# Two experts' gathered rows and a doubled identity moved into buffers that outlive the first stage

## The chip, the cores and the metric

The kernel runs on one core of one Trainium2 chip. A time is device microseconds of one execution. The time before is the median of three timed executions; one more execution was recorded by the hardware profiler, and all rows shown here come from that one.

## The reference

Two blocks follow one another. The first is a recurrent attention (RWKV-7) over 768 steps for 4 batches and 8 heads of width 40; its output is seen as 3072 rows of 320 numbers. The second sends each row to the best of 8 experts, keeps at most 80 rows for an expert (those with the largest gate) and writes the result to the rows' own places.

```python
for t in range(S):
    y[:, :, t] = einsum('bhd,bhde->bhe', rt, state)
    Sa = einsum('bhde,bhe->bhd', state, at)
    state = state * wt - einsum('bhd,bhe->bhde', Sa, bt) + einsum('bhd,bhe->bhde', vt, kt)
...
logits = x @ w_gate
expert_idx = argmax(logits, axis=1)      # gate_w: the softmax value of that expert
for e in range(E):                       # E = 8, capacity = 80
    tok_idx = where(expert_idx == e)[0]  # cut to the 80 largest gate_w
    h = maximum(x[tok_idx] @ w1[e], 0.0)     # 320 -> 1024
    out[tok_idx] = gate_w[tok_idx, None] * (h @ w2[e])   # 1024 -> 320
```

## The kernel before

**First stage.** The recurrence is cut into 24 units (12 blocks of 64 steps, two pairs of batches). For each group of four units a small triangular matrix is inverted in 30 steps; the first group's inversion is done by VectorE, the other five by GpSimd (POOL). The order of all instructions in this stage is written by a planner (`Plan`): each step is given with its engine, a duration, the keys that it reads and writes, and the planner lists the steps greedily by the time at which they could start. Keys such as `("kb", 16)` or `("lt", 5)` name a buffer and the unit or group that uses it. Buffers are rings: `kb` has ten of 1024 columns, so unit 16's is `kb_6`, unit 18's `kb_8`, unit 23's `kb_3`. These ten buffers and a few more belong to the pool `keep`, which lasts until the end. When their units are done, the weights of experts 0 and 1 are loaded into them (`early_weights`, L966 to L982, issued by SyncE, SP): expert 0 uses `kb_4` to `kb_8`, expert 1 `kb_9` and `kb_0` to `kb_3`. Their second layers fill 960 columns of `kb_6`, 640 of `kb_8`, and 640 of `kb_3`. Finished rows of x go to the DRAM tensor `x_rows`.

**Second stage** (L1014 to L1084). The 80 places of each expert are found: `idx_g` (L1077) holds the row numbers for fetching, `idx_s` (L1082) those for writing back. TensorE runs matmuls of no use for the result among this, 22 (`WARM`, L1074) and, behind the last useful one, 16 (`AFTER`, L1084); they read tiles of the pool `sl`.

**Third stage** (L1087 on). The pool `fs` is opened, in memory that the earlier pools gave back. The order in this stage isn't written by hand: each engine's queue is ordered by a list scheduler, which takes an instruction when its operands and its buffer are there by its own estimate, the earlier in the program first. POOL copies the identity twice into `pair` (L1094, L1095), used at L1154. `gather(e)` (L1097) is an indirect DMA issued by POOL that fetches an expert's rows. `turn_x` turns them (two copies `twice` on ScalarE, three transposes on TensorE, the copy `xe` on VectorE), `first_layer` (L1125, L1131) and `second_layer` (L1144) are the matmuls, `turn_y` turns back, scales by the gate that lies in the fetched row's last column (L1156) and scatters by an indirect DMA of POOL (L1157). For each e the program has: `first_layer(e)`, `turn_x(e+1)`, `turn_y(e-2)`, `gather(e+2)`, `second_layer(e-1)`; `gather(0)` to `gather(3)` stand ahead of the loop. The tag `rows` has four buffers, so that `gather(4)` takes that of expert 0.

The weights of experts 2 and 3 are loaded whole by SP (L1004 to L1007) when the first stage ends. Those of experts 4 to 7 follow in ten pieces each (L1177). A piece waits until the piece three before it has landed: SP stores one word of it (`behind`, L1167), and so waits. The fourth piece and all later ones also come after a word of expert 0's fetched rows.

Of the kernel before, what the change touches and what calls it, by code (L numbers as in the profile page):

```python
# [8 lines left out]
F32 = mybir.dt.float32  # L9
# [8 lines left out]
class Plan:  # L18
# [6 lines left out]
    def add(self, eng, us, lag, when, fn, reads=(), writes=(), psum=None, to=(), dma=0.0, sooner=0.0):  # L25
        o = dict(eng=eng, us=us, lag=lag, when=when, fn=fn, i=len(self.ops), deps=set(), psum=None,
                 reads=list(reads), writes=list(writes), to=list(to), dma=dma, sooner=sooner)
        if psum:
            key, n = psum
            if key not in self.width:  # L30
                self.width[key] = n
                o["psum"] = key
            o["writes"].append(key)
        for key in o["reads"]:
            for p, wrote in self.touch.get(key, ()):
                if wrote:
                    o["deps"].add(p)
        for key in o["writes"]:
            for p, _ in self.touch.get(key, ()):
                o["deps"].add(p)  # L40
        for key in o["reads"]:
            self.touch.setdefault(key, []).append((o["i"], False))
        for key in o["writes"]:
            self.touch.setdefault(key, []).append((o["i"], True))
        self.ops.append(o)
# [101 lines left out]
def kernel(  # L147
# [19 lines left out]
    nc = tc.nc  # L167
    B, H, S, D = r.shape
    N, DM = out.shape
    E = moe_w_gate.shape[1]  # L170
    F = moe_w1.shape[2]
    cap = min(int(moe_capacity), N)
    T, C, HB = 64, 32, 64
    NCI = S // T
    NP = B // 2
    NM = NCI * NP
    GU = 4
# [4 lines left out]
    XW = DM + 1  # L182
# [12 lines left out]
    ident = const.tile([128, 128], F32, name="ident")  # L195
# [13 lines left out]
    def view(t, offset, *dims):  # L209
        return bass.AP(t.tensor, t.offset + offset, [list(t.ap[0])] + [list(d) for d in dims])  # L210

    LOOK = 10
# [7 lines left out]
                kb=1024, psi=512, VL=4 * BV, UL=H * X, iv=H * SEG + 1, ivc=512, ends=H * SEG + 1, bT=512, kT=512, rv=1024,  # L220
                lt=C * C, ltT=C * C, gt=512, W=H * X, sT=DM + HB - D, st0=4 * BS, st1=4 * BS, xT=512, xg=GU * XW,
# [4 lines left out]
    keep_ = ctx.enter_context(tc.tile_pool(name="keep", bufs=1))  # L226
    KEPT = [("ah", NM - 10), ("ah", NM - 5), ("ah", NM - 8)] + [("kb", n) for n in range(LOOK)]
    kept = {(n, i % LOOK): keep_.tile([128, COLS[n]], F32, name=f"{n}_{i % LOOK}") for n, i in KEPT}
    weights = {}
    with ExitStack() as p1:  # L230
        hold = p1.enter_context(tc.tile_pool(name="hold", bufs=1))
# [20 lines left out]
        add = plan.add  # L252
# [713 lines left out]
        def early_weights(e):  # L966
            ks = range(NM - 10 + 5 * e, NM - 5 + 5 * e)
            kbs = [at("kb", n) for n in ks]
            rest = at("ah", ks[0])
            w2s = [kbs[2 + i][:, 0 : DM * c].rearrange("p (c d) -> p c d", d=DM) for i, c in enumerate((3, 3, 2))]  # L970
            weights[e] = kbs[0:2], rest, [w2s[f // 3][:, f % 3, :] for f in range(FK)]

            def go():
                for i in range(2):
                    nc.sync.dma_start(kbs[i], moe_w1[e, 128 * i : 128 * i + 128, :])
                for j in range(2):
                    nc.sync.dma_start(rest[64 * j : 64 * j + 64], moe_w1[e, KW:, FH * j : FH * j + FH])
                for i, o in enumerate(w2s):
                    c = o.shape[1]
                    nc.sync.dma_start(o, moe_w2[e, 384 * i : 384 * i + 128 * c, :].rearrange("(c p) d -> p c d", p=128))  # L980
            add("SP", 4.5, 2.0, 0.0, go, [("tops", 0)],
                [("kb", n) for n in ks] + [("ah", ks[0])], dma=7.5)  # L982

        for e in range(2):
            early_weights(e)
        rank_late()
# [100 lines left out]
    fs = ctx.enter_context(tc.tile_pool(name="fs", bufs=2))  # L1087
# [2 lines left out]
    ps_t = ctx.enter_context(tc.tile_pool(name="ps_t", bufs=1, space=PSUM))  # L1090
    ps_y = ctx.enter_context(tc.tile_pool(name="ps_y", bufs=1, space=PSUM))
    rows, xes, hts, yts = {}, {}, {}, {}
    pair = fs.tile([128, HB], F32, name="pair", tag="pair", bufs=1)
    nc.gpsimd.tensor_copy(pair[0:HB], ident[0:HB, 0:HB])  # L1094
    nc.gpsimd.tensor_copy(pair[HB:], ident[HB:, HB:])  # L1095

    def gather(e):  # L1097
        rows[e] = fs.tile([cap, XW], F32, name="rows", tag="rows", bufs=4)
        nc.gpsimd.indirect_dma_start(
            out=rows[e][:, 0:XW], out_offset=None, in_=x_dram[:, :],  # L1100
            in_offset=bass.IndirectOffsetOnAxis(ap=idx_g[:, e : e + 1], axis=0))
# [47 lines left out]
    def turn_y(e):  # L1149
        yT = yts.pop(e)  # L1150
        yq = ps_t.tile([cap, DM], F32, name="yq", tag="yq")
        for i in range(2):
# [6 lines left out]
            in_=y[:, :], element_offset=0, bounds_check=N - 1, oob_is_err=False, in_offset=None)  # L1159

    gather(0)
    words = []

# [6 lines left out]
    for e in range(1, 4):  # L1170
        gather(e)
# [24 lines left out]
    for e in range(E + 1):  # L1196
        if e < E:
            first_layer(e)
        if e + 1 < E:
            turn_x(e + 1)  # L1200
        if e > 1:
            turn_y(e - 2)
            if e + 2 < E:
                gather(e + 2)
        if e > 0:
            second_layer(e - 1)
# [27 lines left out]
```

## Time and profile before

| | us |
|---|---|
| timed executions | 541.29, 542.07, 542.22 (median 542.07) |
| profiled execution, whole | 537.84 |
| its span, first to last instruction | 536.1 |
| TensorE busy, of the span | 406.9 (76%) |
| VectorE busy | 312.1 (58%) |
| GpSimd busy | 225.8 (42%) |
| ScalarE busy | 181.1 (34%) |
| mean granted TensorE clock | 0.902 of full |

The clock has two levels here, 1.0 (2.4 GHz) and 0.5 (1.2 GHz); a value between is a mean over a stretch that has both. Busy shares are means over three stages with different limits. The page's chain of work that ended last reaches back only to the last scatter, so the stages have to be read from the timeline.

### The profile page before, as it was taken

How to read it: one execution, taken by the hardware profiler on the slowest of the kernel's cores; microseconds unless marked ns; L12 is line 12 of the kernel's file. 1: busy time of each engine (PE TensorE's matmuls, PEld its weight loads, DVE VectorE, ACT ScalarE, POOL GpSimd, SP SyncE). 2: the span in 40 equal slices, each digit the busy share in tenths (PEclk: the TensorE clock that was granted, in tenths of full speed). 3: DMA queues.
4: the chain of work that ended last, by engine and by line, in shares of the span. 5: the costliest groups of instructions: out<-in, count | busy, mean ns of one | idle time of the engine just before them, and what ended most of it. 6: DMA issues, size and time to landing. Idle time of an engine off the chain costs nothing. (4 is left out here: it accounts for less than half of the span.)

```text
span 536.1 us, 24562 instructions
## 1 busy us (share of the span) xinstructions
PE 406.9 (76%) x10807; PEld 348.9 (65%) x10807; DVE 312.1 (58%) x706; ACT 181.1 (34%) x353; POOL 225.8 (42%) x395
## 2 busy tenths in 40 slices
PE   2746069987946999898799998989889601699895
PEld 1535058866735877787677877878678501398885
DVE  5867976725720855694575843668567898312212
ACT  2333045453431454346255454343523100010100
POOL 8010011489878701398889930897000000202122
PEclk9988559998975999899999999999979955789999
DMA  9776457667686278567766666333720498676660
GB/s 132 114 112 123 80 132 115 119 101 148 101 237 125 41 175 155 130 129 146 141 153 118 149 152 121 70 75 51 162 73 17 119 321 279 195 220 189 208 199 27
DMA packets 243035, 73.08 MB, mean 136 GB/s; under 512 B 218464, under 2 KB 236272, under 8 KB 242928
## 3 DMA queue, kind: packets, MB, share of 16 engines
q1 hardware_dynamic: 213008, 65.50, 54.2%
q10 hardware_dynamic: 29152, 4.36, 5.3%
q8 instruction: 85, 1.39, 1.1%
q0 software_dynamic: 768, 1.64, 1.1%
q14 instruction: 22, 0.18, 0.1%
HBM read 53.26 MB, written 18.13 MB: 133 GB/s over the span
## 5 line engine op out<-in xcount | busy, mean ns | idle before, releaser
L505 POOL TENSOR_TENSOR tmp<-lt 128x30 f32<-128x30 f32 (+9 forms) x150 | 84.9, 566 | 59.1 <-DMA lt<-blocks 48.4
L507 POOL TENSOR_TENSOR lt<-lt,tmp 128x30 f32<-128x30 f32 (+9 forms) x150 | 90.1, 600 | 11.8
L714 DVE TENSOR_TENSOR UL<-ps,mask 128x832 f32<-128x832 f32 x24 | 24.5, 1021 | 51.9 <-PE ps L709 51.9
L765 PE MATMUL ps<-wsel,xT 128*128 128x192 f32 x192 | 39.1, 349 | 2.3 <-DVE xT L755 1.4
L376 DVE TENSOR_TENSOR_SCAN P<-dec,begins 128x520 f32<-128x520 f32 x24 | 31.5, 1321 | 9.7 <-ACT dec L372 9.6
L351 PE MATMUL ps<-ident,raww 128*128 128x128 f32 x88 | 16.7, 321 | 26.0 <-DMA raww<-in_w_dram 24.8
L765 PEld LDWEIGHTS ps<-wsel,xT 128*128 128x128 f32 x192 | 32.6, 200 | 4.4 <-DVE xT L755 1.7
L351 PE MATMUL ps<-ident,kb 128*128 128x128 f32 x192 | 31.7, 290 | 4.5 <-DVE kb L414 2.6
L742 DVE TENSOR_TENSOR st<-ps,st 128x832 f32<-128x832 f32 (+1 forms) x24 | 23.8, 992 | 18.8 <-PE ps L731 18.7
L492 POOL MEMSET nt<- 32x1024 f32 x12 | 11.3, 945 | 54.6 <-ACT nt L424 54.1
L384 DVE TENSOR_TENSOR_SCAN iv<-dec,ends 128x520 f32<-128x520 f32 x24 | 30.4, 1267 | 4.1 <-ACT ivc L403 3.5
L351 PEld LDWEIGHTS ps<-ident,raww 128*128 128x128 f32 x88 | 11.3, 162 | 28.1 <-DMA raww<-in_w_dram 15.9
L459 DVE TENSOR_TENSOR psi<-ps,mask 128x512 f32<-128x512 f32 x24 | 16.4, 686 | 21.8 <-PE ps L444 20.7
L1157 POOL DMA_INDIRECT out_dram<-y,idx_s x8 | 7.5, 932 | 50.9 <-DVE y L1156 34.9
L618 ACT COPY rv<-ps 128x1024 f32<-128x1024 f32 x24 | 24.4, 1015 | 11.7 <-PE ps L351 11.0
L414 DVE TENSOR_TENSOR kb<-rawkb,ps 128x640 f32<-128x640 f32 x22 | 17.9, 813 | 17.2 <-PE ps L351 11.1
L351 PEld LDWEIGHTS ps<-ident,kb 128*128 128x128 f32 x192 | 22.0, 146 | 8.2 <-issue 3.5
L696 ACT COPY W<-ps 128x832 f32<-128x832 f32 x24 | 20.5, 854 | 14.3 <-PE ps L691 7.4
L731 PE MATMUL ps<-UL,kb 64*64 64x104 f32 (+1 forms) x768 | 23.2, 261 | 2.7 <-DVE UL L714 2.7
L662 PE MATMUL ps<-VL,psi 64*64 64x104 f32 x768 | 24.6, 268 | 0.4 <-DVE VL L635 0.3
L709 PE MATMUL ps<-W,nt 64*64 64x104 f32 x768 | 23.3, 258 | 2.1 <-DVE lb L874 1.9
L351 PE MATMUL ps<-ident,rawr 128*128 128x128 f32 x96 | 16.1, 292 | 10.8 <-DVE ah L394 10.3
(186 smaller groups left out, 951.3 us busy)
## 6 DMA issues: line engine op xcount, KB each, us to landing
w<-in_moe_w_dram SPq DMA_DIRECT2D x16, 320.0 KB
w<-in_moe_w_dram SPq DMA_DIRECT2D x16, 256.0 KB
VL<-in_v_dram SPq DMA_DIRECT2D x96, 40.0 KB
out_dram<-zero SPq DMA_DIRECT2D x8, 480.0 KB
raww<-in_w_dram SPq DMA_DIRECT2D x44, 80.0 KB
rawkb<-in_k_dram SPq DMA_DIRECT2D x44, 80.0 KB
rawkb<-in_b_dram SPq DMA_DIRECT2D x44, 80.0 KB
rawr<-in_r_dram ACTq DMA_DIRECT2D x84, 40.0 KB
```

The costliest lines, as they stand in the source:

```text
L351: nc.tensor.matmul(o, lhsT=i, rhs=ident, start=True, stop=True, is_transpose=True, skip_group_check=True)
L376: nc.vector.tensor_tensor_scan(at("P", n), at("dec", n)[:, 0 : H * SEG], begins, 0.0, op0=Alu.mult, op1=Alu.add)
L384: nc.vector.tensor_tensor_scan(at("iv", n)[:, H * SEG : 0 : -1], at("dec", n)[:, H * SEG : 0 : -1], at("ends", n)[:, H * SEG : 0 : -1], 0. ...
L505: e.tensor_tensor(out=tv, in0=t3[:, 0:s, s : s + 1].to_broadcast([128, s, n]), in1=t3[:, s : s + 1, s + 1 :].to_broadcast([128, s, n]), op ...
L507: e.tensor_tensor(out=t3[:, 0:s, s + 1 :], in0=t3[:, 0:s, s + 1 :], in1=tv, op=Alu.add)
L618: nc.scalar.copy(at("rv", n).rearrange("p (k c) -> p k c", k=2), ps[:, bank(kr) : bank(kr) + 2, :])
L662: nc.tensor.matmul(ps[T * x : T * x + T, b0 + q, X * i : X * i + X], lhsT=psi[rows, q, i, :], rhs=at("VL", n)[rows, vo : vo + X], start=i ...
L709: nc.tensor.matmul(ps[T * bb : T * bb + T, b0 + q, X * i : X * i + X], lhsT=tm[rows, q, i, :], rhs=at("W", n)[rows, wo : wo + X], start=Tr ...
L714: nc.vector.tensor_tensor(out=view(at("UL", n), 0, (M4 * X, 2), (1, M4 * X)), in0=view(ps[:, bank(ku), :], 0, (512, 2), (1, M4 * X)), in1= ...
L731: nc.tensor.matmul(ps[HB * q : HB * q + HB, b0 + bb, yo + lo : yo + hi], lhsT=at("kb", n)[rows, o : o + HB], rhs=at(name, n)[rows, vo + lo ...
L742: nc.vector.tensor_tensor(out=view(st, o, (BS, M4), (step, 2), (1, n_)), in0=view(flat, 512 * bank(ky) + o, (4 * T, M4), (step, 2), (1, n_ ...
L765: nc.tensor.matmul(ps[:, b0, WS * m : WS * m + WX], lhsT=at("xT", n)[:, 2 * T * cof(m, 0) : 2 * T * cof(m, 0) + 2 * T], rhs=wsel_[:, WS * ...
```

## The change

`pair` becomes 64 columns (960 to 1023) of `kb_6`, and the two copies into it become a step of the first stage's plan, on POOL, that reads `("lt", 5)`, the matrix of the last inversion, and writes `("kb", 16)`. It is given to the planner ahead of `early_weights`. The rows of expert 0 are fetched into columns 640 to 960 of `kb_8`, those of expert 1 into the same columns of `kb_3`. Experts 2 to 7 keep the tag `rows` with its four buffers.

```diff
@@ -226,6 +226,7 @@
     kept = {(n, i % LOOK): keep_.tile([128, COLS[n]], F32, name=f"{n}_{i % LOOK}") for n, i in KEPT}
+    pair = kept["kb", (NM - 8) % LOOK][:, 3 * DM : 3 * DM + HB]
     weights = {}
@@ -981,6 +982,12 @@
+        def doubled():
+            for q in range(2):
+                rows_ = slice(HB * q, HB * q + HB)
+                nc.gpsimd.tensor_copy(pair[rows_], ident[rows_, rows_])
+
+        add("POOL", 0.5, 0.1, 0.0, doubled, [("lt", NM // GU - 1)], [("kb", NM - 8)])
         for e in range(2):
             early_weights(e)
@@ -1090,12 +1097,12 @@
     rows, xes, hts, yts = {}, {}, {}, {}
-    pair = fs.tile([128, HB], F32, name="pair", tag="pair", bufs=1)
-    nc.gpsimd.tensor_copy(pair[0:HB], ident[0:HB, 0:HB])
-    nc.gpsimd.tensor_copy(pair[HB:], ident[HB:, HB:])
 
     def gather(e):
-        rows[e] = fs.tile([cap, XW], F32, name="rows", tag="rows", bufs=4)
+        if e < 2:
+            rows[e] = kept["kb", (NM - 6 + 5 * e) % LOOK][0:cap, 2 * DM : 2 * DM + XW]
+        else:
+            rows[e] = fs.tile([cap, XW], F32, name="rows", tag="rows", bufs=4)
```

## Rows read from the trace of the kernel before

**Rows 1.** Busy time in two stretches; then granted clock, DMA share, GB/s.

```profile
460.00:480.00 20.00, 15.23 (x292) 12.74 (x292) 2.64 (x10) 2.34 (x10) 4.32 (x6) 0.83 0.60 188
480.00:500.00 20.00, 18.52 (x492) 17.10 (x487) 3.90 (x10) 1.73 (x7) 3.71 (x4) 1.00 0.62 191
```

**Rows 2.** Timeline from 460 us: start, duration, engine, line; idle before in brackets.

```profile
460.74 0.17 DVE L1077 TENSOR_SCALAR idx_g<-row 80x8 int32<-80x8 f32 x1
460.84 2.76 PE L1084 MATMUL ids_p<-sel,ones_b 128*128 128x384 bf16 x16
463.83 0.23 POOL L1094 COPY pair<-ident 64x64 f32<-64x64 f32 x1 [18.98 <-PE ids_p L1084]
...
464.69 1.13 POOL L1099 DMA_INDIRECT rows<-x_rows,idx_g  x1 [0.36 <-POOL pair L1095]
```

**Rows 3.** Waits of 440 to 537 us: total, times, longest.

```profile
POOL pair L1094 <- PE ids_p L1084: 19.0, 1, 19.0
```

**Rows 4.** Timeline: first transposes, first layer of expert 0, that of expert 3.

```profile
467.69 0.50 PE L1110 MATMUL xp<-ident,rows 80*128 80x80 f32 x2 [4.09 <-DMA rows<-x_rows,idx_g]
...
469.00 4.11 PE L1125 MATMUL hp<-xe,kb 128*64 128x80 f32 x64 [0.50 <-DVE xe L1113]
...
488.58 2.39 PE L1125 MATMUL hp<-xe,w 128*64 128x80 f32 x63
```

**Rows 5.** Timeline: VectorE's result and the indirect DMA that waits for it.

```profile
492.60 0.55 DVE L1156 TENSOR_SCALAR y<-yq,rows 80x320 f32<-80x320 f32 x1
...
493.42 0.94 POOL L1157 DMA_INDIRECT out_dram<-y,idx_s  x1 [5.73 <-DVE y L1156]
```

**Rows 6.** Short stretches, as Rows 1: the last three columns are clock, DMA share, GB/s.

```profile
462.50:463.00 0.50, 0.50 (x5) 0.31 (x4) 0.00 (x0) 0.00 (x0) 0.00 (x0) 1.00 0.46 164
...
465.00:466.00 1.00, 0.00 (x0) 0.00 (x0) 0.00 (x0) 0.00 (x0) 0.82 (x1) 0.84 0.00 0
466.00:467.00 1.00, 0.00 (x0) 0.00 (x0) 0.00 (x0) 0.00 (x0) 0.87 (x1) 0.50 0.33 96
...
472.00:473.00 1.00, 1.00 (x24) 0.94 (x20) 0.00 (x0) 0.00 (x0) 0.00 (x0) 0.74 0.53 125
```

**Rows 7.** The tile `rows`: the eight gathers' time from issue to landing.

```profile
DMA to landing us min/median/max: 2.9/4.1/4.7
```

**Rows 8.** Timeline: last use of unit 16's keys; POOL around the last inversion's end.

```profile
341.45 0.89 PE L731 MATMUL ps<-UL,kb 64*64 64x104 f32 x32
...
373.03 0.16 POOL L519 MEMSET lt<- 128x32 f32 x1
384.66 0.21 POOL L816 COPY xg<-gsm 128x4 f32<-128x4 f32 x1 [11.47 <-DVE gsm L813]
```

**Rows 9.** Timeline: early weights' issue; last expert's weights and the matmuls that use them.

```profile
424.96 2.31 SPq L980 DMA_DIRECT2D kb<-in_moe_w_dram  x3
...
516.79 0.22 SPq L1167 DMA_DIRECT2D word<-w1r  x1
...
521.82 1.12 PE L1131 MATMUL hp<-xe,w1r 64*64 64x80 f32 x32
```

**Rows 10.** Stretches near the end of the first stage, columns as Rows 6.

```profile
388.00:390.00 2.00, 0.43 (x15) 0.46 (x19) 1.10 (x6) 0.19 (x1) 0.00 (x0) 1.00 0.34 54
390.00:392.00 2.00, 2.00 (x73) 1.80 (x66) 1.90 (x9) 0.28 (x1) 0.00 (x0) 0.65 0.97 329
```

**Rows 11.** Timeline: matmuls of L1074, behind L1070 in the program, ahead of it here.

```profile
453.89 4.36 PE L1074 MATMUL warm<-sel,ones_b 128*128 128x384 bf16 x13
```

**Rows 12.** Timeline: ScalarE's queue, and the second layer that needs its result.

```profile
491.48 0.39 ACT L1107 COPY twice<-rows 80x64 f32<-80x64 f32 x2 [7.11 <-DMA rows<-x_rows,idx_g]
...
491.78 0.44 ACT L1134 ACTIVATE hT<-hp 128x320 f32<-128x320 f32 x1
...
500.38 2.77 PE L1144 MATMUL yp<-hT,w 128*64 128x80 f32 x71
...
507.80 0.39 ACT L1107 COPY twice<-rows 80x64 f32<-80x64 f32 x2 [7.52 <-DMA rows<-x_rows,idx_g]
```

## Prediction, made before the changed kernel was run

> **What bounds the kernel now.** The page comes first, but its chain of work that ended last stops at the last scatter, and its busy shares are means over three stages. So I cut the span into stretches and looked for the ones that the change touches. In the expert stage TensorE is the limit once it runs: it is busy 18.52 of 20 us from 480 on, and only 15.23 of 20 between 460 and 480, at a mean clock of 0.83 [rows 1]. Time lost at that stage's start is lost at the end too, since everything behind it is TensorE's own work. The timeline of the start shows the loss. The row numbers `idx_g` are ready at 460.74 + 0.17 = 460.91 us, yet the first gather starts at 464.69 [rows 2]. POOL stands before it in `pair`'s first copy, which begins at 463.83, right behind the 16 last idle matmuls (460.84 + 2.76 = 463.60) [rows 2]; the view of waits books POOL's idle time there on these matmuls [rows 3]. `pair` lies in memory given back by the pool that the matmuls read. TensorE then stands idle 4.09 us for the fetched rows, and begins expert 0's first layer at 469.00. That layer takes 4.11 us for 64 matmuls, where expert 3's takes 2.39 for 63 [rows 4]: it runs at the lower clock.
>
> **The change part by part.**
>
> *The copies leave the front of the gather, and rows 0 and 1 no longer lie in `fs`.* Then `gather(0)` waits only for `idx_g` (and for weights in `kb_8`, below). When POOL waits for a VectorE result with an indirect DMA, it starts 493.42 − (492.60 + 0.55) = 0.27 us behind it [rows 5]. So the gather starts at 460.91 + 0.27 = 461.18 instead of 464.69: 3.51 us sooner. From its start to the first transposes it took 467.69 − 464.69 = 3.00 us; the same gives 464.18, later than TensorE's own 463.60, so TensorE doesn't cap it. Gain 3.51, if the gather lands as fast.
>
> *Does it land as fast?* The weights of experts 2 and 3 and three pieces fill the DMA engines until about 462.75 (share 0.46 in the half microsecond from 462.5). The old gather's bytes move only after 466.0, over 1.3 us behind its start (share 0 from 465 to 466) [rows 6]; 461.18 + 1.3 is 462.5, so the new ones meet a quarter of a microsecond of that traffic. Bounds: nothing, or the spread of the eight gathers, 4.7 − 2.9 = 1.8 us, where the slow ones ran beside weights [rows 7]. A gain has no place, since 2.9 is the fastest of the eight. I take 0.2, near the lower end, because nearly all traffic is gone by then. The Trainium skill ("DMA: Bandwidth & Descriptors", Issuing engines are not separate DMA queues) says that DMAs of all issuing engines share the same 16 engines and interleave; it speaks against starting a gather into a weight load. By that rule the landing would be a slow one, and the sum 3.4 us instead of 5.0: rival B.
>
> *The clock.* TensorE's clock was full through the 16 matmuls, fell between 465 and 466, some 2 us after they ended, and came back between 472 and 473 [rows 6]. With the transposes at 464.2 to 464.4, the idle stretch behind 463.60 shrinks from 4.09 to about 0.7 us, and the first layer, 1.31 us behind the transposes [rows 4], starts near 465.6, where the clock fell before. I take it that it stays: 4.11 − 2.39 = 1.7 us more. Bounds: nothing (it falls all the same, at worst with the loss of now) to 1.7.
>
> *The two copies in the first stage.* Two of 0.23 us [rows 2] with their issue are some 0.5 us of POOL. They wait for the last inversion's end (373.03 + 0.16 = 373.19) and for unit 16's readers (341.45 + 0.89 = 342.34, long done); behind them on POOL stands the copy L816, which VectorE releases only at 384.66 after 11.47 us of idle time [rows 8]. That idle time hides them; without it they would cost 0.5 us of a queue that nobody waited for. In the plan they keep nobody else's step from its time, so I cost the planner's order at nothing. They pass L816, L819, the two clears of `la`, and POOL's constants of the second stage; none reads `pair`.
>
> *New waits.* SP's `early_weights(0)` must follow the copies: it is issued near 425 [rows 9], over 50 us later. Should overlaps be tracked by buffer, `gather(0)` also waits for the weights in `kb_8`, issued at 425 as well, some 36 us before it. Both cost nothing.
>
> *Buffers.* With rows 0 and 1 elsewhere, four buffers serve experts 2 to 5, so `gather(4)` and `gather(5)` needn't wait for a finished expert and may come right behind `gather(3)`. `gather(2)`, the first in `fs`, still has to wait for 463.60; in POOL's queue its turn comes at 461.18 + 1.13 + 0.31 + 0.91 + 0.30, about 463.8, so that wait is hidden. Cost and gain: none I can see, since TensorE works through.
>
> *What is late next?* SP resumes the weight pieces when rows 0 have landed, 3.3 us sooner, but TensorE 5.0 us sooner: the margin shrinks by 1.7. For the last expert `w1r` has landed by 516.79 and is used at 521.82 [rows 9], a margin of 5.0, so 3.3 are left. The gathers 6 and 7 move with TensorE.
>
> *Sum.* 3.5 − 0.2 + 1.7 = 5.0 us. The profiled execution, 537.84 us with a span of 536.1, would come to 532.8. It lies 4.2 us below the median of the timed ones (542.07), for reasons that it can't show; I carry the difference over: 542.07 − 5.0 = 537.0.
>
> **The rivals.**
>
> *B, the start is sooner but half of the rest is lost.* Either the clock falls at its old place, 465.7 or so, when TensorE has done little since 463.60, and the first layer is slow as now: gain 3.3. For it: between 388 and 390 TensorE was busy 0.43 of 2 us and full work followed at once, yet the clock went down in the next stretch [rows 10]; a short thin stretch is enough. Against: there the thin stretch was longer than the 0.7 us here. Or the weights, which may end later in a timed execution, hold the gather back by 1.8: gain 5.0 − 1.6 = 3.4, and with the clock lost too, 1.7. So 538.7 for either, 540.4 for both. The Trainium skill ("TensorE: Matmul & The Clock Gate", Part 1) says that the monitor's phase isn't tied to the kernel's start and that the clock's steps shift from run to run; by that the clock is kept in some executions and lost in others. One profile can't show that.
>
> *C, the gather still waits for the idle matmuls*, through a wait that I don't see. Then only the copies are gone: it starts 0.27 behind 463.60, at 463.87, a gain of 0.8 us, and the clock falls as before: 541.3. For it: POOL's queue is ordered by a scheduler. Against: `kb_8` isn't in the memory that those matmuls read.
>
> *D, ScalarE's queue turns against it.* The order of this stage is made by readiness, not by the program: 13 of the matmuls of L1074 run ahead of L1070's, which precede them in the text [rows 11]. With rows 4 and 5 there early, the copies `twice` of experts 4 and 5 can be queued sooner, and that of expert 6 becomes the next candidate. ScalarE works its queue in order: already `twice` of expert 4 stood 7.11 us at its head, with expert 3's Relu (491.78) right behind it. The point from which it decides: if `twice` of expert 6 gets ahead of expert 3's Relu, the second layer of expert 3 (500.38) must wait for rows 6, which land at 507.80 [rows 12], and for copies and Relu: 507.80 + 0.39 + 0.44 − 500.38 = 8.3 us. Net 8.3 − 5.0 = 3.3 us slower: 545.4. One place later, ahead of expert 4's Relu, it costs nothing. Against: by readiness the Relu comes long before rows 6 can be asked for.
>
> **How the numbers follow.** Forecast A (sooner and clock kept) 0.60; B 0.24; C 0.08; D 0.08. The predicted time is A's, 537.0. A's own span: 0 to 0.7 us of extra landing, and the timed ones' spread (541.29 to 542.22), give 535.9 to 537.9. The range reaches from there over B, to 540.3, and leaves out C and D. A change of 0.2%, 1.1 us, is about what a measurement of this kernel can tell from none. A and B are faster by more (0.83, B's worst end nearly so), C is within it (0.09), D slower (0.08).
>
> **What would show each step.** In the changed kernel's timeline: POOL's two copies near 373 us; no POOL work between `idx_g` and the first gather, which starts 0.2 to 0.4 us behind it; transposes 3.0 to 3.3 us later; the clock 1.0 from 459 on and the first layer in 2.4 us; gathers 4 and 5 behind gather 3; TensorE as dense as before from the second expert on. A slower landing or a slow first layer is B; a gather behind 463.6 is C; a Relu held by `twice` of expert 6 is D. The prediction is wrong altogether if the first stage's length moves, which I hold fixed, or if the 4.2 us between profile and timing belong to the stretch in question.

## The result, and the profile after

Timed beside one another, the changed kernel has a median of 536.72 us in 20 executions (529.54 to 542.08), the kernel before 541.55 us in 20 (537.34 to 545.42). The ratio given is 0.9865 with a 95% interval of 0.9836 to 0.9894; on the 542.07 us shown that is 534.8 us. The forecast was 537.0 with a range from 535.9, so the measured gain, 7.3 us, is larger than the range allowed. The rule behind this ratio and the later ones leaves out executions more than 1.5% above their kernel's fastest, here 9 of the changed kernel's 20 and one of the other's, while the medians given are of all executions. Those of all 20 differ by 4.8 us (0.991).

The profiled execution of the changed kernel took 534.31 us, with a span of 532.6; the one before 537.84 and 536.1. The two stretches of [rows 1], in the changed kernel, then two short ones; the last three columns are granted clock, DMA share and GB/s:

```profile
460.00:480.00 20.00, 16.65 (x307) 13.42 (x305) 2.85 (x11) 2.69 (x12) 5.66 (x6) 0.91 0.70 210
480.00:500.00 20.00, 20.00 (x551) 19.12 (x548) 5.00 (x12) 1.59 (x5) 3.23 (x4) 1.00 0.63 188
...
468.00:469.00 1.00, 0.00 (x0) 0.00 (x0) 0.00 (x0) 0.00 (x0) 0.69 (x2) 1.00 0.99 342
...
473.00:474.00 1.00, 1.00 (x20) 1.00 (x17) 0.00 (x0) 0.00 (x0) 0.00 (x0) 0.50 0.40 104
```

TensorE gained in both stretches: 16.65 for 15.23 busy us in the first, and 20.00 for 18.52 in the second, where I had expected nothing. But from 468 to 469 it does nothing at all while the DMA engines are full, and five microseconds later its clock stands at the lower level. The timeline shows both, beside the start that [rows 2, 4] show of before:

```profile
461.07 0.17 DVE L1084 TENSOR_SCALAR idx_g<-row 80x8 int32<-80x8 f32 x1
461.17 2.76 PE L1091 MATMUL ids_p<-sel,ones_b 128*128 128x384 bf16 x16
461.53 1.13 POOL L1106 DMA_INDIRECT kb<-x_rows,idx_g  x1 [15.26 <-DVE idx_s L1089]
...
464.38 0.27 SPq L1174 DMA_DIRECT2D word<-kb  x1
464.50 0.33 PE L1117 MATMUL xp<-ident,kb 80*128 80x80 f32 x2 [0.57 <-DMA kb<-x_rows,idx_g]
464.70 1.77 SPq L1184 DMA_DIRECT2D w<-in_moe_w_dram  x4
465.72 2.25 PE L1132 MATMUL hp<-xe,kb 128*64 128x80 f32 x51 [0.50 <-DVE xe L1120]
...
469.08 0.37 PE L1132 MATMUL hp<-xe,kb 128*64 128x80 f32 x3 [1.12 <-issue]
469.82 0.23 PE L1132 MATMUL hp<-xe,kb 128*64 128x80 f32 x1 [0.36 <-issue]
470.54 0.56 PE L1132 MATMUL hp<-xe,kb 128*64 128x80 f32 x9 [0.49 <-issue]
...
473.40 3.49 PE L1132 MATMUL hp<-xe,kb 128*64 128x80 f32 x63
```

The gather starts 461.53 − 461.24 = 0.29 us behind `idx_g` (3.78 before), and the transposes 464.50 − 461.53 = 2.97 us later, as in the forecast. The first layer begins at the full clock and runs 51 of its 64 matmuls in 2.25 us. Then TensorE stops for nothing that the profile shows ("issue": no operand, buffer or semaphore is late), three times, 1.97 us in all, while its granted clock is still 1.00, and the last 13 matmuls are spread from 469.08 to 471.1. Expert 1's first layer, at 473.40, runs at half the clock: 3.49 us for 63 matmuls, where [rows 4] have 2.39. The waits of the whole last stage:

```profile
PE yp L1151 <- issue: 2.0, 4, 0.6
PE hp L1132 <- issue: 2.0, 3, 1.1
```

The copies stand where they were expected, behind the last inversion's final clear, with 8.98 us of idle POOL behind them (11.47 in [rows 8]):

```profile
376.63 0.16 POOL L520 MEMSET lt<- 128x32 f32 x1
376.69 0.55 POOL L988 COPY kb<-ident 64x64 f32<-64x64 f32 x2
386.22 0.19 POOL L817 COPY xg<-gsm 128x4 f32<-128x4 f32 x1 [8.98 <-issue]
```

Two queues of the last stage changed beyond what the diff says. POOL issues gathers 4 and 5 right behind gather 3 (starts at 0.29, 1.73, 3.55, 4.76, 5.97 and 7.18 us behind `idx_g`). And SP issues the first three weight pieces of expert 4 behind the word of rows 0, as the burst of four at 464.70; in the kernel before they go out ahead of that word:

```profile
449.20 5.34 SPq L1177 DMA_DIRECT2D w<-in_moe_w_dram  x3
```

### The profile page after: what moved, and what is told of

Its sections match the earlier page's. It is cut to its first block, busy times and chain, and to the rows that moved or that the text cites. A ratio compares the mean times of both kernels' runs of the same rounds, so it can differ in the third digit from the quotient of the medians.

```text
span 532.6 us, 24559 instructions
## 1 busy us (share of the span) xinstructions
PE 407.0 (76%) x10807; PEld 349.6 (66%) x10807; DVE 314.2 (59%) x706; ACT 181.5 (34%) x353; POOL 223.4 (42%) x395
## 5 line engine op out<-in xcount | busy, mean ns | idle before, releaser
L508 POOL TENSOR_TENSOR lt<-lt,tmp 128x30 f32<-128x30 f32 (+9 forms) x150 | 88.2, 588 | 11.8
L715 DVE TENSOR_TENSOR UL<-ps,mask 128x832 f32<-128x832 f32 x24 | 24.5, 1023 | 51.0 <-PE ps L710 51.0
L710 PE MATMUL ps<-W,nt 64*64 64x104 f32 x768 | 24.4, 263 | 2.0 <-DVE lb L875 1.4
```

The source lines that it names most:

```text
L508: e.tensor_tensor(out=t3[:, 0:s, s + 1 :], in0=t3[:, 0:s, s + 1 :], in1=tv, op=Alu.add)
L710: nc.tensor.matmul(ps[T * bb : T * bb + T, b0 + q, X * i : X * i + X], lhsT=tm[rows, q, i, :], rhs=at("W", n)[rows, wo : wo + X], start=Tr ...
L715: nc.vector.tensor_tensor(out=view(at("UL", n), 0, (M4 * X, 2), (1, M4 * X)), in0=view(ps[:, bank(ku), :], 0, (512, 2), (1, M4 * X)), in1= ...
```

## Where the time went, expert by expert

Three pairs of traces were taken apart in the same way: from `idx_g` to expert 0's first layer, then from each expert's first layer to the next, then to the end (all from the starts in the timelines). The second and third pair are of one chip each; of the first the chip isn't known. Gains in us:

| pair | up to first layer | experts 0, 1 | 2, 3 | 4, 5 | 6 | last | sum |
|---|---|---|---|---|---|---|---|
| the two first profiles | 3.61 | −2.83 | 2.64 | 0.08 | −0.06 | 0.39 | 3.83 |
| before_again, after_third (chip 3) | 3.43 | −4.16 | 2.67 | 0.28 | 0.00 | 0.05 | 2.27 |
| before_third, after_fourth (chip 15) | 3.47 | −2.66 | 2.37 | −0.07 | 0.14 | 0.06 | 3.31 |

So the stretch in question gained 2.3 to 3.8 us, where 5.0 was forecast: the start came as forecast, experts 0 and 1 lost what the clock should have given and more, and experts 2 and 3 gained what nobody had asked for. That the first profile came out 537.84 − 534.31 = 3.5 us faster, not far from the forecast's 5.0, is no confirmation: a gain and a loss of about 2.7 us, neither of them forecast, cancel in it.

The rest of an execution, the 456 to 465 us ahead of `idx_g`, differs from run to run by more than the change is worth. The same kernel's `idx_g` was ready at 461.24, 456.43, 457.53 and 462.67 us in four traces of the changed kernel, at 460.91, 460.56 and 462.96 in three of the kernel before.

## The experiments

Theory: the gathers, which the change moves, keep TensorE from issuing its matmuls wherever it works beside them (the expectations call that waiting for its own instructions; the traces show the waits, not their inside). Rivals: the weight pieces at their new place do that; the clock alone does; ScalarE's queue does (rival D at another place). The clock alone can't, since the waits of the first layer come while it is still full (1.00 up to 472 in the first profile after). "`idx_g` to the end" is the length compared, since the stage ahead of it varies. Expert 0's first layer always waits 0.50 us for `xe`; in some traces the profile books that as "issue", though the copy ends 0.06 us ahead of the layer there as everywhere. The issue waits given here leave it out.

**The copies without the rows** (rows of experts 0 and 1 stay in `fs`).

```diff
+    pair = kept["kb", (NM - 8) % LOOK][:, 3 * DM : 3 * DM + HB]
+        add("POOL", 0.5, 0.1, 0.0, doubled, [("lt", NM // GU - 1)], [("kb", NM - 8)])
         rows[e] = fs.tile([cap, XW], F32, name="rows", tag="rows", bufs=4)
```

> Only the doubled identity is moved into the first stage; all gathered rows stay in the late pool with four buffers. Theory of the prediction (start): the first gather then waits for the end of the 16 idle matmuls, starts about 0.3 us behind them and gains 0.8 us; ratio 0.998 to 0.999, 74.4 us from idx_g to the end. Theory of the loop (gathers 4 and 5 leave it): the same here, since they stay in it. Theory of the plan (the new step shifts the first stage): the ratio of the whole change, 0.987.

Measured: 537.46 against 537.86 us, ratio 1.0001 (0.9967 to 1.0036). POOL and TensorE in its timeline:

```profile
463.51 2.76 PE L1091 MATMUL ids_p<-sel,ones_b 128*128 128x384 bf16 x16
...
467.27 1.13 POOL L1103 DMA_INDIRECT rows<-x_rows,idx_g  x1 [19.93 <-PE ids_p L1091]
```

The gather waits for the idle matmuls now, since `fs` lies in the memory that they read, and starts 467.27 − 466.27 = 1.00 us behind them; before it was 464.69 − 463.60 = 1.09 with two copies between [rows 2]. The copies had been hidden in the time that an indirect DMA takes to start behind TensorE. So moving the copies alone gives 0.1 us, and the rest takes the rows' new place too. Moving the rows alone wasn't run: the copies, ahead of the gather in POOL's queue, would still wait for the matmuls there. (Rival C had 0.27 us here and so a gain of 0.8; it is 0.1.)

**The changed kernel again.** The runs from pair_only down to six_buffers were on one chip, number 3.

> The changed kernel once more, for a second profile and a ratio beside the others. Both theories expect about 0.987 of before, and about 71 us from the end of idx_g to the end of the span (75.2 before, 71.4 in the first profile after).

> The changed kernel for a third trace. If TensorE waits for its instructions on this chip: 71.3 us from idx_g to the end, the first two experts 14.2 to 14.4 us. If not: expert 0 takes 4.2 us and expert 1 5.8, as in the kernel with pieces first; the gain over the kernel before on the same chip is then the sum predicted, 3.5 + 1.7 = 5.2 us, 64 to 65 us, unless the last expert's weights come late: TensorE is then 5 us further ahead of them than before, whose margin was 5.0, and 65 to 67 us are left.

Measured, in two groups of runs: 534.84 us against 537.86, ratio 0.9927 (0.9885 to 0.9969), and 533.04 against 538.57, 0.9900 (0.9845 to 0.9955); `idx_g` to the end 71.17 and 71.97 us. Both show the three issue waits in the first layer, 2.0 and 2.1 us, and the lower clock behind them. In the first the full clock was back for expert 1 (5.78 us from its first layer to the next), in the second not (7.09).

**The kernel before against itself.**

> The kernel before once more, for a second trace on the same chip as the three others of this call. Ratio 1.000. Two kinds of traces have been seen: one in which TensorE waits some 1.2 to 1.5 us for its own instructions beside each gather in the loop, and one without these waits. In the first kind: 75 us from idx_g to the end and the experts 2 to 5 at 7.8 to 8.5 us from first layer to first layer, as before; in the second kind 69 to 70 us, the experts at 6.6 to 6.7.

Measured: 536.23 against 538.57 us, 0.9936 (0.9889 to 0.9982): the interval leaves out 1 for a kernel that is the same. That is the size of error with which every ratio here has to be read. `idx_g` to the end is 74.24 us, 0.95 from the first profile's 75.19.

**Only two fetched early, all buffers of the loop kept** (experts 4, 5 take the same columns again, two buffers in `fs`; gathers 4 to 7 stay in the loop).

```diff
-        if e < 2:
+        if e % 4 < 2:
-            rows[e] = fs.tile([cap, XW], F32, name="rows", tag="rows", bufs=4)
+            rows[e] = fs.tile([cap, XW], F32, name="rows", tag="rows", bufs=2)
```

> The change with its buffers undone: experts 0 and 4 share the columns of kb_8, 1 and 5 those of kb_3, and the late pool has two buffers, so that gathers 4 and 5 again wait for finished experts. Theory of the start: all of the gain stays, ratio 0.987 to 0.991, 70 to 71 us from idx_g to the end. Theory of the loop: TensorE's stalls come back, experts 2 and 3 take 7.9 and 8.1 us from first layer to first layer instead of 6.8 and 6.6, some 2.6 us of the gain are lost: ratio 0.991 to 0.996, 73 to 74 us.

> The change with its buffers undone, as in the kernel loop_kept. If TensorE waits for its instructions on this chip: 70.7 us again, 0.6 less than the changed kernel. If not: the same as the changed kernel within 0.7 us, since gathers 4 and 5 then cost nothing at either place.

Measured: 532.21 us against 537.86, ratio 0.9908 (0.9875 to 0.9942), and 533.55 against 538.57, 0.9894 (0.9833 to 0.9956); `idx_g` to the end 70.69 and 73.29. The four weight pieces come as in the changed kernel, but gathers 4 and 5 don't, and the first layer has no issue wait, where the changed kernel has 2.0 us. Gather 3 alone, 0.3 us into the layer as in the changed kernel, causes none:

```profile
466.08 2.64 PE L1132 MATMUL hp<-xe,kb 128*64 128x80 f32 x64 [0.50 <-issue]
466.37 0.91 POOL L1106 DMA_INDIRECT rows<-x_rows,idx_g  x1 [0.30 <-issue]
```

In the first trace expert 0 takes 4.67 us instead of 5.8: the clock's gain is real. Experts 2 to 5, each with a gather beside it, take 7.8 to 8.4. So the length of 70.69 is what the theory of the start expects, but by a trade: experts 0 and 1 win 3.8 us against the changed kernel's trace `again`, experts 2 and 3 lose 2.6. The second trace shows rival D's mechanism, at expert 2 (POOL, ScalarE, TensorE):

```profile
462.66 0.91 POOL L1106 DMA_INDIRECT rows<-x_rows,idx_g  x1 [0.91 <-PE ids_p L1091]
...
469.02 0.39 ACT L1114 COPY twice<-rows 80x64 f32<-80x64 f32 x2 [5.11 <-DMA rows<-x_rows,idx_g]
469.31 0.42 ACT L1141 ACTIVATE hT<-hp 128x320 f32<-128x320 f32 x1
469.79 0.70 PE L1151 MATMUL yp<-hT,kb 128*64 128x80 f32 x13 [2.44 <-ACT hT L1141]
```

Rows 2, asked for beside the four weight pieces, took 469.02 − 462.66 = 6.4 us where rows 0 took 3.0 to be used. `twice` of expert 2 stood at ScalarE's head for 5.11 us with expert 0's Relu behind it, and TensorE stood still for 2.44 us; expert 0 took 6.68 us and expert 1 7.43, together 3.7 us more than in the first trace. The Trainium skill ("DMA: Bandwidth & Descriptors", Issuing engines are not separate DMA queues) says that DMAs of all issuing engines share the same engines and interleave; the trace agrees here, with 6.4 us, though not for rows 0, which met nothing.

**More buffers in the kernel before** (rows stay in `fs`, gathers 4 and 5 come early).

```diff
-        rows[e] = fs.tile([cap, XW], F32, name="rows", tag="rows", bufs=4)
+        rows[e] = fs.tile([cap, XW], F32, name="rows", tag="rows", bufs=6)
```

> The kernel before with six buffers for the gathered rows and nothing else: the first gather is as late as before, but gathers 4 and 5 can go right behind gather 3. Theory of the start: no change, ratio 0.999 to 1.001, 75 us from idx_g to the end. Theory of the loop: experts 2 and 3 take 6.6 to 6.8 us instead of 7.9 and 8.1, ratio 0.994 to 0.996, 72 to 73 us.

Measured: 534.64 against 537.86 us, ratio 0.9957 (0.9919 to 0.9995); `idx_g` to the end 72.35, where pair_only beside it has 73.92 and before_again on the same chip 74.24. Experts 4 and 5 take 6.66 and 6.62 us instead of about 7.8 to 8.5, and expert 0 6.50 instead of 5.8, with 0.3 us of issue waits. The expectation named experts 2 and 3 for this gain and was wrong there: with six buffers gathers 6 and 7 wait only for experts 0 and 1, so they stand beside experts 2 and 3 (7.86 and 7.90 us), and it is the stretches of 4 and 5 that have no gather. Here nothing of the start changed, and SP's pieces kept their place: moving two gathers away from working matmuls is worth 1.6 to 1.9 us alone.

**Another chip: extra gathers, all gathers early, pieces ahead, all apart.** loop_extra is the changed kernel with a fetch, into the buffer of rows that are done, added to three experts' stretches; all_early has six buffers for experts 2 to 7; pieces_first puts the three pieces back ahead of the word; quiet issues all gathers, then a word of rows 7, then the pieces, six in flight.

```diff
 # loop_extra, in the loop
+            if e in (2, 3, 6):
+                nc.gpsimd.indirect_dma_start(out=rows[e - 2][:, 0:XW], ...)
 # all_early
+            rows[e] = fs.tile([cap, XW], F32, name="rows", tag="rows", bufs=6)
 # pieces_first
-    behind(rows[0][0:1, 0:1])
     def piece(dst, src):
+        if len(landed) == IN_FLIGHT:
+            behind(rows[0][0:1, 0:1])
```

> The changed kernel with three more gathers that nobody reads: behind the results of experts 0, 1 and 4 in POOL's queue, into the buffers of rows that are done. Theory of the loop (a gather issued while TensorE works keeps it waiting for its own instructions): the experts 2, 3 and 6 take 7.9 to 8.2 us from first layer to first layer instead of 6.8, 6.6 and 6.6, and the stretch from idx_g to the end grows from 71.3 to about 75 us. Rival (those experts were slow in the kernel before because of rows that came late): no change, 71.3 us, since nothing waits for the added gathers.

> The changed kernel with six late buffers, so that gathers 6 and 7 also go ahead of the loop. Theory of the loop: experts 4 and 5 take 6.6 us each instead of 8.4 and 7.9, 3.1 us less; theory of crowding: two more gathers in the first layers cost there what they save, as 4 and 5 did, so 70.5 to 71.5 us from idx_g to the end. Without crowding: 68.2 us.

> The changed kernel with SP's order of before: three weight pieces go ahead of the word of expert 0's rows instead of behind it. Theory of the start as predicted: the pieces run beside the first gather, which lands 0.2 us later (at most 1.8): transposes 3.4 us behind idx_g instead of 3.25, and no other difference. Theory of crowding (weight pieces beside gathers 4 and 5 starve TensorE in the first layers): the flood of four pieces at the start of the first layer becomes three or less, the first two experts take 13 to 14 us instead of 14.2 to 14.4, 70.5 to 71.3 us from idx_g to the end.

> All eight gathers ahead of the loop (six late buffers), and all paced weight pieces behind the landing of expert 7's rows, with six in flight instead of three so that they catch up. Theory of crowding: with no weight traffic beside the gathers the first two experts take 10.5 to 11 us instead of 14.2 to 14.4, and all others 6.6: 64.5 to 66 us from idx_g to the end, ratio 0.980 to 0.984, if the pieces arrive in time. If the gathers alone starve TensorE: the first two take 14 us or more, 68 to 71 us.

Measured, against 538.06 us of the kernel before on this chip:

| | us | ratio (interval) | `idx_g` to end | experts 0 to 6 | last to end |
|---|---|---|---|---|---|
| loop_extra | 532.96 | 0.9964 (0.9923 to 1.0005) | 71.00 | 5.21 5.78 6.68 6.55 7.03 6.59 8.52 | 20.17 |
| all_early | 530.44 | 0.9901 (0.9857 to 0.9945) | 68.85 | 4.44 5.78 6.68 6.55 6.55 6.55 8.83 | 18.96 |
| pieces_first | 531.98 | 0.9924 (0.9874 to 0.9974) | 66.02 | 4.16 5.79 6.67 6.55 6.55 7.48 7.86 | 16.53 |
| quiet | 530.56 | 0.9883 (0.9794 to 0.9973) | 66.44 | 4.15 5.79 6.67 6.55 6.55 6.55 7.57 | 18.18 |

On this chip (number 0) TensorE has hardly any issue waits (0.3 us in loop_extra, none in the others). pieces_first has the same six gathers ahead and beside the first layer as the changed kernel, and runs through:

```profile
464.91 2.43 PE L1132 MATMUL hp<-xe,kb 128*64 128x80 f32 x64 [0.50 <-DVE xe L1120]
...
465.24 0.91 POOL L1106 DMA_INDIRECT rows<-x_rows,idx_g  x1 [0.30 <-issue]
...
466.45 0.90 POOL L1106 DMA_INDIRECT rows<-x_rows,idx_g  x1 [0.30 <-issue]
```

That was a miss for the theory in its plain form: an extra gather costs experts 2 and 3 nothing here (6.68 and 6.55 us). What binds instead is the last weights. In loop_extra, all_early and quiet TensorE waits 2.2, 3.2 and 1.8 us for them (and in loop_extra 1.7 us for the rows of expert 7); in pieces_first, which has three pieces ahead, no such wait is left (experts 6 and 7 wait 1.7 us for their rows).

**The pieces ahead, on a chip with the waits.**

> The changed kernel with three weight pieces ahead of the word of expert 0's rows, as in the kernel before, once more. Theory of late weights: the pieces of the last expert are then three pieces, some 4 us, further on than in the changed kernel, so where TensorE doesn't wait for its instructions this one is 1 to 3 us faster than the changed kernel (66.0 us from idx_g to the end in its first trace). Theory of crowding: it is faster only where TensorE does wait for them, by up to 1 us.

Measured on chip 3: 532.96 against 538.57 us, 0.9888 (0.9839 to 0.9937); `idx_g` to the end 69.41, against 71.97 of the changed kernel beside it. The issue waits stay, 2.0 us in the first layer and 1.6 in the loop, though the first layer now meets its pieces one by one; so the flood of four isn't their cause. The same kernel had none on chip 0. What differs is the clock behind them. First pieces_first_2 from 468 us, then the changed kernel (after_third), whose first layer began 4.3 us earlier, from 464:

```profile
468.00:470.00 2.00, 0.79 (x11) 0.54 (x7) 0.00 (x0) 0.39 (x2) 1.48 (x2) 1.00 0.88 228
470.00:472.00 2.00, 1.24 (x35) 0.92 (x38) 0.00 (x0) 0.00 (x0) 0.00 (x0) 1.00 0.80 226
472.00:474.00 2.00, 1.82 (x54) 1.57 (x48) 0.81 (x2) 0.74 (x3) 0.00 (x0) 1.00 0.88 265
```

```profile
464.00:466.00 2.00, 0.52 (x7) 0.28 (x6) 0.00 (x0) 0.34 (x2) 1.32 (x2) 1.00 0.95 318
466.00:468.00 2.00, 1.35 (x15) 0.96 (x18) 0.00 (x0) 0.05 (x1) 0.00 (x0) 0.62 0.58 150
468.00:470.00 2.00, 2.00 (x39) 1.64 (x41) 0.66 (x2) 0.61 (x3) 0.00 (x0) 0.50 0.05 18
```

TensorE has little to do in both, 0.79 and 0.52 busy of 2 us, and then 1.24 and 1.35; the clock stays at 1.00 in the one and falls to 0.50 in the other, and experts 0 and 1 take 12.86 against 15.70 us. Whether the order of SP or chance keeps the clock, one trace can't tell. In time the two kernels are level (0.9888 and 0.9900).

**Which of the two starves TensorE?** On a third chip (15), the kernel before, the changed one, one with half the gathers, and one with both moves.

```diff
 # few_gathers
     def gather(e):
+        if e > 3:
+            rows[e] = rows[e - 4]
+            return
 # both_moved: pieces_first, and
+            rows[e] = fs.tile([cap, XW], F32, name="rows", tag="rows", bufs=6)
```

> The kernel before, for the trace of this chip. Both theories: idx_g to the end takes 74 to 75.5 us if TensorE waits for its own instructions beside the gathers here (experts 2 to 5 at 7.8 to 8.5 us), and about 70 us if it doesn't on this chip (then 6.55 to 6.8 each).

> The changed kernel beside the one before on one chip. If the losses of its first layer (2.0 us of instruction waits) and at experts 4 and 5 (1.3 us each) belong to the gathers that lie there, they show where the kernel before shows 7.8 to 8.5 us an expert, and not at all where it shows 6.6: idx_g to the end 71 to 72 us in the first case, about 66 in the second.

> Experts 4 to 7 compute on the rows fetched for experts 0 to 3, so four of the eight gathers are left out and the output of these experts is not the reference's. Theory 1 (TensorE waits for its instructions because of the gathers): no instruction wait over 0.6 us in the first layer, expert 0's period 4.2 to 4.8 us unless rows 2 come late, and experts 2 to 6 at 6.55 to 6.8 us each; idx_g to the end 66 to 68 us. Theory 2 (because of the weight pieces): the waits of 2 us in the first layer stay, since the four pieces come where they come in the changed kernel, and experts 4 and 5 stay at 7.8 to 8.5 us; 70 to 72 us. On a chip that shows no such waits in the kernel before, it tells nothing.

> The changed kernel with the first three pieces back ahead of the word of rows 0 and with six buffers for rows, so that all gathers come behind one another at the start. Theory 1: the first layer waits 2 to 3 us for instructions beside the gathers, and every expert from 1 on takes 5.8 to 6.8 us; idx_g to the end 67 to 68 us, 3 us less than the changed kernel, a ratio of about 0.985 to 0.99 to the kernel before. Theory 2: the first layer waits less (under 1 us) since three pieces lie elsewhere, but experts 4 and 5 stay at 7.8 us or more. On a chip without the waits the last expert's weights become the limit, 1 to 2 us, and it gains nothing over the changed kernel with the pieces first.

Measured: `idx_g` to the end 73.74 us for the kernel before, 70.43 for the changed one, 70.72 with few gathers (531.2 against 537.51 us, ratio 0.9866, 0.981 to 0.9922) and 71.88 with both moved (536.93 us, 0.99, 0.9812 to 0.9988). This chip shows the waits. The first gather of the loop in the kernel before, and the second layer beside it:

```profile
488.68 0.92 POOL L1099 DMA_INDIRECT rows<-x_rows,idx_g  x1 [0.30 <-issue]
489.42 0.44 PE L1144 MATMUL yp<-hT,kb 128*64 128x80 f32 x6 [0.35 <-issue]
...
490.17 0.41 PE L1144 MATMUL yp<-hT,kb 128*64 128x80 f32 x5 [0.30 <-issue]
```

TensorE stops 0.4 us behind the gather's start, gets six matmuls, stops again, gets five more: 80 matmuls take 490.58 − 486.37 = 4.2 us. In the changed kernel, without a gather there, they take 3.0:

```profile
491.85 3.00 PE L1151 MATMUL yp<-hT,w 128*64 128x80 f32 x80
```

The kernel before has eight such waits in the last stage, two for each of the four gathers in the loop:

```profile
PE yp L1144 <- issue: 2.8, 8, 0.4
```

With four gathers left out, one wait of 0.2 us is left in the loop and none in the first layer (the 0.5 is the wait for `xe`), though the four weight pieces come as in the changed kernel:

```profile
PE hp L1135 <- DMA w<-in_moe_w_dram: 3.2, 2, 2.4
...
PE hp L1135 <- issue: 0.5, 1, 0.5
PE yp L1154 <- issue: 0.2, 1, 0.2
```

Experts 0 to 5 take 4.80, 5.78, 6.68, 6.55, 6.55 and 6.99 us. With all eight gathers at the start, they meet in the first layer:

```profile
465.01 2.01 PE L1132 MATMUL hp<-xe,kb 128*64 128x80 f32 x50 [0.50 <-issue]
466.20 0.91 POOL L1106 DMA_INDIRECT rows<-x_rows,idx_g  x1 [0.30 <-issue]
467.41 0.91 POOL L1106 DMA_INDIRECT rows<-x_rows,idx_g  x1 [0.30 <-issue]
468.24 0.37 PE L1132 MATMUL hp<-xe,kb 128*64 128x80 f32 x4 [1.22 <-issue]
...
468.62 0.91 POOL L1106 DMA_INDIRECT rows<-x_rows,idx_g  x1 [0.31 <-issue]
469.68 0.30 PE L1132 MATMUL hp<-xe,kb 128*64 128x80 f32 x2 [1.06 <-issue]
469.84 0.91 POOL L1106 DMA_INDIRECT rows<-x_rows,idx_g  x1 [0.30 <-issue]
471.09 0.23 PE L1132 MATMUL hp<-xe,kb 128*64 128x80 f32 x1 [1.11 <-issue]
```

One to four matmuls run between waits of over a microsecond, 4.2 us of waits in five (the 0.50 ahead of the layer left out); behind this thin stretch the clock is down at 0.50 from 472 on, and expert 0 takes 10.95 us. Experts 2 to 6 take 6.55 to 6.74. So the waits go where the gathers go, on the chips that show them: in the first profiles and on chips 3 and 15, each of the 36 gathers in a loop has two. Two limits belong to this. In the loop each gather starts about 1.2 us behind a scatter, which is an indirect DMA of POOL as well. Scatters with no gather behind them, over sixty in these traces, show two waits in all (0.44 us in loop_kept, 0.2 in few_gathers), so a scatter alone doesn't do it; a gather without a scatter wasn't tried there. And in the first layer gather 3 alone causes none, gathers 3, 4 and 5 together do. My length for few_gathers, 66 to 68 us, was missed all the same: TensorE, unhindered, runs into the last expert's weights.

```profile
511.56 1.46 PE L1135 MATMUL hp<-xe,w 128*64 128x80 f32 x32 [2.40 <-DMA w<-in_moe_w_dram]
513.80 2.71 PE L1135 MATMUL hp<-xe,w 128*64 128x80 f32 x32 [0.78 <-DMA w<-in_moe_w_dram]
```

It waits 3.2 us there, and its clock falls to 0.50 (2.71 us for 32 matmuls); expert 6 takes 9.17 us and the last one 19.74, against 6.75 and 16.30 in the kernel before. both_moved missed its 67 to 68 us too, by the clock: I had counted the waits of the first layer and not what follows from them.

## Why the prediction was right or wrong

- **The start: right.** 0.29 us behind `idx_g` and 2.97 to the transposes, for 0.27 and 3.00; 3.4 to 3.6 us of gain where 3.51 − 0.2 were written. The contention of 0.2 us didn't come. pair_only shows that the copies' move alone gives 0.1 us of it. Rival C's condition is absent. One reading on the way was wrong and cost nothing that shows: `gather(2)`'s wait for the idle matmuls isn't hidden behind its turn in the queue at about 463.8; it starts at 464.79, 0.9 us behind their end.
- **The copies at nothing: right.** They run at 376.69, hidden by 8.98 us of idle POOL.
- **The clock, 1.7 us: the mechanism right, the sum wrong.** It is full when the first layer starts, and where TensorE isn't starved the term is there: expert 0 took 4.16 us in pieces_first on chip 0 and 4.67 in loop_kept, against 5.8. In the changed kernel on the chips with the waits it fell later, behind the starved stretch, and experts 0 and 1 lost 2.7 to 4.2 us. The Trainium skill ("TensorE: Matmul & The Clock Gate", Part 1) says that the clock's steps shift from run to run; the trace agrees: the same kernel's expert 1 took 6.95, 5.78, 7.09 and 5.79 us in four traces.
- **"Cost and gain: none I can see, since TensorE works through": the step that failed.** I named the move of gathers 4 and 5 and costed it at nothing, because I looked for operands. But TensorE didn't work through: in [rows 1] it is busy 18.52 of 20 us from 480 on, and the missing 1.5 us were the waits beside the gathers (2.9 us for "issue" over the stage in the first profile). Moved away they gave 2.4 to 2.7 us at experts 2 and 3; at their new place they cost the first layer some 2 us, and the clock behind it. few_gathers shows that it is the gathers, six_buffers that they cost this in the kernel before as well.
- **"SP resumes the weight pieces … 3.3 us sooner": failed too.** I held SP's order fixed. The first three pieces now come after the word of rows 0 instead of ahead of it, so the weights land later, not sooner. I gave the last expert's `w1r` a margin of 3.3 us, down from 5.0 [rows 9]; the word that follows its landing is at 518.09, and the layer at 518.72, so 0.6 is left:

```profile
516.37 2.42 PE L1132 MATMUL hp<-xe,w 128*64 128x80 f32 x64
...
518.09 0.22 SPq L1174 DMA_DIRECT2D word<-w1r  x1
518.72 0.62 PEld L1138 LDWEIGHTS hp<-xe,w1r 64*64 64x64 f32 x32
```

  It cost nothing yet in this trace, but it is the limit that few_gathers, loop_extra, all_early and quiet (whose pieces come later still) ran into.
- **Rival D: its mechanism is real, its place was wrong.** Not expert 6's `twice` but expert 2's stands ahead of a Relu, expert 0's, and it stood there in the kernel before too (470.22 and 473.87 us in its timeline). In the changed kernel (469.27 and 471.86) it costs nothing, because the first layer is late itself; in loop_kept_2, where rows 2 come late and the layer doesn't, it costs 2.44 us.
- **Why the measured time lies below the range: the spread was mis-sized, and the rest is open.** I took the spread of three executions, 541.29 to 542.22, for all the noise there is. Twenty spread over 8 us for the kernel before and 12.5 for the changed one, and the kernel against itself gave 0.9936. The traces account for 2.3 to 3.8 us of the 7.3, the medians of all executions for 4.8. Nothing in the traces answers to the rest: the instructions of the first stage stand in the same order but for the two copies, the three weight pieces go out later, and `idx_g` varies within either kernel by more than it differs between them. The planned copies by themselves bring nothing: pair_only has them and is level with the kernel before (1.0001). Whether the first stage is a little shorter in the mean stays open.

What stays open besides: why gathers hold up TensorE on chips 3 and 15 and not in the four traces of chip 0, and what it is that TensorE lacks there. The kernel before has no trace on chip 0, so what the change is worth there isn't shown.

## What to carry to other kernels

When a buffer is freed or added, list every instruction that a scheduler may now move, and look at each queue: here two gathers and three weight pieces moved, and these moves were worth 2 to 4 us each way, beside the 3.5 us that the edit was made for. Look for "issue" waits of TensorE next to gathers before calling it busy, and put gathers where it stands idle anyway. And measure a kernel against itself before reading a ratio of half a per cent.

## What the runs showed of the hardware that I had not expected

- Gathers, indirect DMAs of GpSimd, hold up TensorE's matmuls on chips 3 and 15, though they share no operand: mostly two waits of 0.3 to 0.6 us beside one gather in the loop, 1.2 us of an expert's time, and waits of over 1 us each where gathers follow one another (4.2 us in both_moved). On chip 0 eight gathers in a row (quiet) cost nothing. The Trainium skill ("Runtime: NRT & Kernel Launch", Instruction fetch mechanics) says that each engine's sequencer fetches its instructions ahead through a DMA queue of its own, mostly hidden. If the waits are this fetch, it isn't hidden beside gathers; no run here shows the fetch itself.
- An indirect DMA starts 0.3 us behind a VectorE result, but 0.9 to 1.0 us behind the end of the matmuls that it waits for (`gather(2)` of the changed kernel, pair_only), by ends of matmuls that the profile models. With two copies between them it had been 1.09, so those cost 0.1.
- Ahead of the last stage, the same instructions take between 456.4 and 464.5 us.
